# Four interleaved attention layers on one core: the keys of the first full layer made inside the layer, block by block

## The chip, the cores and the metric

The kernel runs on one core of one Trainium2 chip. The metric is the device time of one execution in microseconds (us); the time before is the median of three runs, 2756.83 us (2756.65 to 2759.04).

The engines are named by what they do: TensorE (PE in the profile) multiplies matrices into PSUM, ScalarE (ACT) takes the exps, VectorE (DVE) moves results out of PSUM and does small arithmetic, GpSimd (POOL) masks and squares, SyncE (SP) issues every transfer between memory and the core's own SBUF.

## What is computed

Four layers in turn, each a layer norm, an attention and a residual sum on x of 2048 rows by 512. Layers 0 and 2 (weights A) attend to a window of 256 keys, layers 1 and 3 (weights B) to all 2048. There are 32 heads of 16 columns.

```python
def layer(x, wqkv, wo, window):          # the reference, cut
    h = layernorm(x)
    q, k, v = heads(h @ wqkv)            # 32 heads x 2048 x 16
    scores = einsum("hqd,hkd->hqk", q, k) * 16 ** -0.5
    if window:
        scores = where(0 <= i - j < 256, scores, -1e9)
    return x + merge(softmax(scores) @ v) @ wo
x = layer(x, A_wqkv, A_wo, True)         # layer 0
x = layer(x, B_wqkv, B_wo, False)        # layer 1
x = layer(x, A_wqkv, A_wo, True)         # layer 2
x = layer(x, B_wqkv, B_wo, False)        # layer 3
```

## The kernel before

**Tiles.** The 2048 rows are four chunks of 512 (`NQ`, index c). The 32 heads are eight quads of four (`NQD`, index qd); two quads are one head tile of 128 columns (`NHT` = 4, index t or ht). Attention takes one quad and one chunk of queries at a time. In a full layer that is 16 key steps of two exps each (`attn_full`); a step's scores go to PSUM (line 727), ScalarE takes the exp (L735), and the value products follow a step or two later (L779). In a windowed layer it is three steps of two exps (`attn_win`, L731 and L812).

**Where operands lie.** Projected keys and queries go to scratch in memory (kf for full layers, kw for windowed ones, qs for queries), and attention loads them from there: qt, the queries of a quad, at L748, and kt, its keys in two halves, at L752. One row of each is a shift that keeps the exp in range. It comes from sums of squares: a projected tile is squared on GpSimd (sq, L521), a small matmul adds the squares by head (`squares`), and from that come, for keys, a maximum per chunk (km, L562) and then one shift row per head over all four chunks (mk in `key_shift`, L602), for queries the rows m (L575, L576). So a quad's attention needs its keys of all four chunks with their shift, and its queries with theirs.

**Side work.** All projections of later chunks and layers run as side work between attention steps. A `Work` is a generator with a cost and what it depends on; a `Side` holds the list for a stretch, paces it against the number of steps, and `finish()` runs whatever is left. A whole projection of keys, queries, values or outputs of a chunk is 48 matmuls of 128x512, four tiles of twelve; one head tile's keys or queries ("a quarter") are twelve; values of half the heads are 24 of 128x512 in work. In a full layer the pools leave one PSUM tile, b, for all side work, each matmul is split into eight small ones of 64x32, and VectorE evicts it in two passes (`join`). `share` doles out side work there: a budget per step, and a lag that falls by 0.42 us a step, with at most two matmuls at a time. `soon`, `drain` and `pend` order what VectorE does after a tile.

**The order of the work.** TensorE's order is the order of the code; in full layers VectorE's too. SyncE issues its transfers in the order in which the scheduler put them, each once what it reads is there and its buffer is free. Qt has two buffers, kt three halves.

**Layer 0 to 1, before.** Side work in layer 0 makes all keys of layer 1 for chunks 0 to 2 and the queries of chunk 0 (`side0`). The tail after layer 0's last attention (`tails`, `lasts`) makes the queries of chunk 1, the keys of chunk 3 and what is left of the values. Then `key_shift` writes the shift of all heads, and layer 1 runs its 32 quads (chunk by chunk, eight quads each) without a block in which anything of layer 1 has to be waited for, but for the upper half of the values, due before quad 4 of chunk 0. Layer 3 already does otherwise: it goes by head tiles, and in each block of two quads makes the next head tile's keys and queries (K3, Q3, shift3).

Of the kernel before, what the change touches and what calls it, by code (L numbers as in the profile page):

```python
# [19 lines left out]
P = 128  # L20
# [169 lines left out]
def fast_path(ctx, tc, flag, a_x, a_wqkv, a_wo, b_wqkv, b_wo, out):  # L190
# [21 lines left out]
    WT, ST, pend = {}, {}, []  # L212
    VQ, vt_ = [deque() for _ in range(4)], [0.0]
# [15 lines left out]
    def soon(chain, us, f):  # L229

        if PH["full"]:
            VQ[chain].append((clock[0], us, f))
        else:
            f()

    def drain(upto=None):

        if upto is not None:
            for q in VQ[:upto]:
                while q:  # L240
                    vec(q[0][1])
                    q.popleft()[2]()
            return
        while vt_[0] <= clock[0] + 0.2:
            q = next((q for q in VQ if q), None)
            if q is None:
                return
            vec(q[0][1])
            q.popleft()[2]()
# [179 lines left out]
    def norm(l, c, xs, tail=False):  # L429

        mv, y, nb, out = ST[l, c][1], [], [], []

        def scales():
            y.append(rsqrt(nc, vp, f"{l}_{c}", mv[:, :, 1]))
# [4 lines left out]
        def parts(i):  # L439
            xn = vp.tile([P, D], F32, name=f"xn{l}_{c}_{i}", tag="xn", bufs=1)  # L440
# [201 lines left out]
    def wo(l, c, tail):  # L642
# [4 lines left out]
        for i in range(4):  # L647
# [11 lines left out]
            yield -MM if PH["full"] else -12 * MM  # L659
        if PH["full"]:  # L660
            yield from norm(l + 1, c, xs, tail)

    def wo_part(c, t):
# [6 lines left out]
        for i in range(4):  # L670
# [7 lines left out]
            nc.sync.dma_start(out[0, k * P:(k + 1) * P, :] if t == NHT - 1 else xd[k], xs[i])  # L678
            yield -MM

    def epilogue(l, c, qd, a):
# [25 lines left out]
        def parts():  # L707
            o = vp.tile([P, QC], F32, name=f"o{n}", tag="o", bufs=1)
            nc.vector.transpose(o, OT.pop(t).rearrange("p b u d -> p (b u d)"))
            hl = O[l, c, t] = wp.tile([P, 2, QC], F16, name=f"oh{n}", tag="ohl", bufs=OB)  # L710
# [4 lines left out]
        if u:  # L715
            soon(1, 1.2, parts)
# [103 lines left out]
    class Work:  # L820
# [34 lines left out]
        proj = property(lambda self: self.name is not None and self.name[0] in ("K", "Q", "K3", "Q3"))  # L855
# [27 lines left out]
    class Side:  # L883
# [65 lines left out]
        def share(self):  # L949

            self.budget = min(self.budget + max((self.cost - self.spent) / max(self.steps - 3 - self.k, 1), self.least), 0.75)
            self.lag = max(self.lag - 0.42, -0.3)
# [5 lines left out]
            while (self.q and clock[0] >= PH["free"] and self.budget >= MM / 2 and (self.lag < 0.25 or self.budget > 0.45)  # L958
                   and self.spent - s0 < 1.5 * MM):
# [26 lines left out]
    def attention(l, works):  # L986
# [5 lines left out]
        for t in range(NHT if l == 3 else 1):  # L992
            for c in range(NQ):
                qds = range(2 * t, 2 * t + 2) if l == 3 else range(NQD)
                if l == 1:

                    sd = sd or Side(NT * NQD // 2, works[0], works[1], 0.33)
                    while ("Q", 1, c) not in DONE:
                        sd.one(True)
                    settle()  # L1000
                else:
                    sd = Side((3 if win else NT) * len(qds), works[t * NQ + c], works[t * NQ + c + 1], 0.34 if l == 3 and t < 2 else 0.0)
                ops = load(l, c, qds[0])
                for qd in qds:
                    if (l, c, qd) == (1, 0, NQD // 2):
                        sd.finish()
                        sd = Side(NT * NQD * NQ - NT * NQD // 2, works[1], works[2], 0.33)
                    nxt = load(l, c, qd + 1) if qd + 1 in qds else None
                    a = acc[qd % 2 if win else 0]
                    began, u = clock[0], 0  # L1010
# [22 lines left out]
                if l != 1 or c == NQ - 1:  # L1033
                    sd.finish(l == 3 and (t, c) != (NHT - 1, NQ - 1))
                if not win:
                    settle()
# [14 lines left out]
    def K3(c, ht, act=False):  # L1051
        return Work(later(keys, 3, c, act, ht), PK / 4, ("K3", c, ht), [("T", 3, c)], True, ring=not act)

    def Q3(c, ht, act=False, after=()):
        return Work(later(queries, 3, c, act, ht), PK / 4, ("Q3", c, ht), [("T", 3, c), *after], True, ring=not act)

    def shift3(ht):
        def gen():
            key_shift(3, ht)
            yield -1e-6  # L1060
        return Work(gen(), 0.0, ("S3", ht), [("K3", c, ht) for c in range(NQ)])
# [81 lines left out]
    def side0(c):  # L1143
# [4 lines left out]
        if c == 2:  # L1148
            return [F(*[(kf, True, k, k + 1) for k in range(NQ)]), K(0, 3), OO(0, 1), Q(0, 3), VV(0, 3), K(1, 0), T(1, 1)]
        return [F(*[(qs[1, k], False) for k in range(NQ)]), K(1, 1), OO(0, 2), VV(1, 0, True, (0,)), T(1, 2), K(1, 2), Q(1, 0)]  # L1150

    def side2(c):
        if c == 0:
            return [OO(1, 3), Q(2, 2), T(2, 3), K(2, 3)]
        if c == 1:
            return [OO(2, 0), Q(2, 3), T(3, 0), K3(0, 0, True)]
        if c == 2:
            return [OO(2, 1), VV(2, 3), T(3, 1), K3(1, 0, True)]
        return [OO(2, 2), T(3, 2), K3(2, 0, True)]
# [5 lines left out]
    def side1():  # L1165
        m = [(ty, s) for ty in range(2) for s in range(4)]
        a = [CW(*x, [("C", *y)] if y else [("Q", 1, 2)]) for y, x in zip([None] + m, m)]
        a += [Q(1, c, False) for c in (2, 3)]
        for c in range(3):
            a += [OO(1, c), T(2, c)] + ([Q(2, c - 1, False)] if c else []) + [K(2, c, False), VV(2, c, False)]  # L1170
        return a

    def side3(t, c):
        a = [Q3(c + 1, t)] if c < 3 else []
        if t < 3:
            a.append(K3(c, t + 1))
            if c == 3:
                a += [shift3(t + 1), Q3(0, t + 1)]
# [6 lines left out]
    works = [[side0(c) for c in range(NQ)], [[upper(1, c) for c in range(3)], side1()], [side2(c) for c in range(NQ)],  # L1185
             [side3(t, c) for t in range(NHT) for c in range(NQ)]]
    late = lambda l: [("N", l, 3)]
    tails = {0: [VV(1, 2, True, (0,)), OO(0, 3, True), VV(1, 1, True, (0,), late(1)), Q(1, 1, True, late(1)), T(1, 3), K(1, 3)],
             2: [VV(3, 0, True, (0,)), OO(2, 3, True), VV(3, 1, True, (0,), late(3)), VV(3, 2, True, (0,), late(3)), Q3(0, 0, True, late(3)), T(3, 3), K3(3, 0, True)]}
    lasts = {0: [VV(1, 3)], 2: [VV(3, 3, True, (0,)), VV(3, 0, True, (1,))]}  # L1190
    for l in range(4):
        if l % 2 == 0:
            attention(l, works[l] + [tails[l]])
            all_of(tails[l], lasts[l])
            key_shift(l + 1, 0 if l else None)
# [45 lines left out]
```

## Time and profile before

| | us |
|---|---|
| median of three runs | 2756.83 |
| the profiled execution, own time | 2759.5 |
| its span | 2757.7 |
| TensorE busy (91%) | 2496.1 |
| ScalarE busy (86%) | 2362.9 |
| VectorE busy (40%) | 1094.9 |
| GpSimd busy (19%) | 515.8 |

The profile is one execution; its own time lies 1.8 us above its span, and 2.7 us above the median. Layer 0's attention runs from 54 to 437 us of the span, its tail to 495.5; layer 1 to 1447; layer 2 to 1727 and its tail to 1783.6; layer 3 to 2738. Rows of the timeline give start, length, engine, line, operation, tiles and in brackets the idle time before it and what ended it; "x12" are twelve instructions merged. A busy TensorE is not at its peak, since matmuls overlap; what one costs is read from start to start.

### The profile page before, as it was taken

What the parts mean: (1) busy time and instruction counts of PE and PEld (TensorE: products, weight loads), DVE (VectorE), ACT (ScalarE), POOL (GpSimd) and SP (SyncE); (2) the same over time, 40 slices, a digit from 0 to 9 for tenths busy, and PEclk for the clock granted to TensorE, in tenths of its full rate; (3) what the DMA queues carried; (4) which work ended last, traced back from release to release, by engine and by line L of the source; (5) the groups of instructions that cost most, each with busy time, mean ns of one, the idle gap of its engine ahead of it and who ended that gap; (6) DMA issues with size and microseconds to landing.
All of it is one profiled execution on the core that took longest, in us unless ns stands there. A gap on an engine that the chain in (4) does not pass through costs nothing.

```text
span 2757.7 us, 112292 instructions
## 1 busy us (share of the span) xinstructions
PE 2496.1 (91%) x50513; PEld 1100.3 (40%) x50513; DVE 1094.9 (40%) x2314; ACT 2362.9 (86%) x2683; POOL 515.8 (19%) x1074
## 2 busy tenths in 40 slices
PE   7888989999989999999998898899899999998987
PEld 3233334444433344444443333534444444433332
DVE  5564554122343335325326566323333333333333
ACT  4556654899999999999995667399999999999997
POOL 1445552001000000100105678100000000000000
PEclk9999999999999999999999999999999999999999
DMA  8888856322342224324225565623232333333332
GB/s 286 226 241 240 244 178 191 96 83 82 100 120 79 86 93 137 102 78 126 93 73 169 157 181 143 175 72 109 84 107 90 98 97 104 112 104 123 114 120 103
DMA packets 335035, 359.67 MB, mean 130 GB/s; under 512 B 113616, under 2 KB 250320, under 8 KB 328144
## 3 DMA queue, kind: packets, MB, share of 16 engines
q1 hardware_dynamic: 334544, 352.40, 42.3%
q8 instruction: 397, 6.50, 1.0%
q14 instruction: 94, 0.77, 0.1%
HBM read 239.60 MB, written 96.99 MB: 122 GB/s over the span
## 4 chain that ended last, share of the span: by engine, by line
ACT 56%; PE 23%; issue 11%; DVE 5%; DMA 3%; POOL 2%; SPq 0%; ACTq 0%; DVEq 0%; POOLq 0%
ACT e L735 55%; PE b L402 10%; PE acc L812 3%; PE acc L779 3%; PE bs L402 2%; PE s L731 2%; PE s L727 2%; PE b L399 1%; POOL e L802 1%; POOL e L805 1%; DMA qt<-qs 1%; DMA kt<-kw 0%; DMA wr<-in_A_wo_dram 0%; DVE ot L694 0%; DMA w<-wd 0%
## 5 line engine op out<-in xcount | busy, mean ns | idle before, releaser
L735 ACT ACTIVATE e<-s 128x1024 f32<-128x1024 f32 (+2 forms) x2432 | 2238.8, 1058 | 121.0 <-PE s L731 95.3
L779 PE MATMUL acc<-e,vt 64*17 64x512 f32 x16384 | 1085.0, 590 | 1.3 <-issue 1.3
L727 PE MATMUL s<-qt,kt 64*32 64x512 f16 x16384 | 849.0, 380 | 130.4 <-ACT e L735 106.6
L727 PEld LDWEIGHTS <-kt 64*32 64x32 f16 x16384 | 406.7, 89 | 944.2 <-issue 868.8
L779 PEld LDWEIGHTS acc<-e,vt 64*17 64x17 f32 x16384 | 280.5, 92 | 61.1 <-issue 1.5
L805 POOL TENSOR_SCALAR_AFFINE_SELECT e<-e 128x256 f32<-128x256 f32 x512 | 224.9, 446 | 196.5 <-ACT e L735 195.4
L802 POOL TENSOR_SCALAR_AFFINE_SELECT e<-e 128x256 f32<-128x256 f32 x448 | 198.1, 449 | 114.1 <-ACT e L735 112.3
L712 POOL TENSOR_TENSOR oh<-o,oh 128x512 f16<-128x512 f32 x31 | 36.1, 1165 | 938.1 <-DVE oh L711 884.8
L812 PE MATMUL acc<-e,vt 128*17 128x384 f32 (+2 forms) x2816 | 204.7, 396 | 5.3 <-POOL e L802 4.0
L731 PE MATMUL s<-qt,kt 64*128 64x384 f16 (+2 forms) x1408 | 129.0, 280 | 64.0 <-ACT e L735 38.2
L415 DVE TENSOR_SCALAR sa<-acc 128x512 f32<-128x512 f32 x64 | 44.3, 692 | 335.4 <-PE acc L779 335.4
L402 PE MATMUL b<-xc,w 128*128 128x512 f16 x696 | 166.1, 390 | 7.0 <-DMA w<-wd 5.8
L677 DVE SCALAR_TENSOR_TENSOR x<-b,x 128x512 f32<-128x512 f32 x122 | 83.9, 688 | 193.0 <-PE b L399 189.8
L402 PEld LDWEIGHTS <-w 128*128 128x128 f16 x816 | 77.4, 100 | 122.8 <-issue 35.8
L521 POOL TENSOR_TENSOR sq<-sp 128x512 bf16<-128x512 f16 x28 | 41.0, 1463 | 442.2 <-DVE sp L515 427.6
L506 ACT ACTIVATE sp<-b 128x512 f16<-128x512 f32 x58 | 34.7, 598 | 103.3 <-PE b L402 91.2
L731 PEld LDWEIGHTS <-kt 64*128 64x128 f16 x1408 | 54.4, 94 | 167.6 <-issue 137.0
L521 POOL TENSOR_TENSOR sq_h<-sp_h 128x512 bf16<-128x512 f16 x27 | 40.1, 1484 | 409.8 <-DVE sp_h L515 409.8
L399 PE MATMUL b<-wo,oh 64*32 64x512 f16 x2592 | 109.9, 376 | 6.2 <-DVE x L677 3.1
L399 PE MATMUL b<-xc,w 64*32 64x512 f16 x2688 | 110.9, 376 | 3.0 <-DVE j L416 2.3
L399 PE MATMUL b<-xc,w_h 64*32 64x512 f16 x2592 | 104.4, 376 | 4.1 <-DVE km L562 3.9
L415 DVE TENSOR_SCALAR j_h<-b 128x512 f32<-128x512 f32 x27 | 18.7, 691 | 218.7 <-PE b L399 187.6
(136 smaller groups left out, 1874.8 us busy)
## 6 DMA issues: line engine op xcount, KB each, us to landing
kt<-kf SPq DMA_DIRECT2D x128, 512.0 KB
qt<-qs SPq DMA_DIRECT2D x128, 256.0 KB
xd<-x SPq DMA_DIRECT2D x96, 256.0 KB
x<-xd SPq DMA_DIRECT2D x96, 256.0 KB
w<-wd SPq DMA_DIRECT2D x22, 1024.0 KB
kt<-kw SPq DMA_DIRECT2D x64, 256.0 KB
qs<-sp SPq DMA_DIRECT2D x48, 256.0 KB
wo<-wd SPq DMA_DIRECT2D x12, 1024.0 KB
```

The costliest lines, as they stand in the source:

```text
L399: nc.tensor.matmul(ps[g:g + 32, r], a[k, g:g + 32], b[k], start=(i == 0), stop=(i == len(pairs) - 1), skip_group_check=True)
L402: nc.tensor.matmul(ps, a, b, start=(i == 0), stop=(i == len(pairs) - 1))
L415: nc.vector.tensor_scalar(dst, ps[0], scale, None, op0=ALU.mult)
L521: nc.gpsimd.tensor_tensor(sq, sp[:, 0], sp[:, 0], ALU.mult)
L677: nc.vector.scalar_tensor_tensor(xs[i], p, 1 / WS, xs[i], op0=ALU.mult, op1=ALU.add)
L727: nc.tensor.matmul(ps[g:g + 32, h], kt[R * h:R * h + R, pr, kc + g:kc + g + 32], qt[R * h:R * h + R, pr], start=True, stop=True, skip_grou ...
L731: nc.tensor.matmul(ps[:, h, s0:s0 + wd_], kt[R * h:R * h + R, pr, kc:kc + P], qt[R * h:R * h + R, pr, qc:qc + wd_], start=True, stop=True)
L735: nc.scalar.activation(e[:, :, w0:w1], ps[:, :, w0:w1], AF.Exp, scale=SCALE)
L779: nc.tensor.matmul(acc[r][32 * h:32 * h + DH + 1, :], V[l, qd // 4, j // 8][k, j % 8, 4 * (qd % 4) + h, :], es_[h // 2][k, h % 2, :], star ...
L802: nc.gpsimd.affine_select(v, v, pattern=[[0, 2], [-1, P]], compare_op=ALU.is_gt, fill=0.0, base=0, channel_multiplier=1)
L805: nc.gpsimd.affine_select(v, v, pattern=[[0, 2], [1, P]], compare_op=ALU.is_ge, fill=0.0, base=0, channel_multiplier=-1)
L812: nc.tensor.matmul(a[32 * h:32 * h + DH + 1, q * P:(q + nb) * P], V[l, (4 * c + j) // 4][:, j % 4, 4 * qd + h, :], es_[h // 2][:, h % 2, s ...
```

## The change

- Layer 0's side work makes only head tile 0 of layer 1's keys (KH), and only head tile 0 of the queries of chunk 0 (QH). The tail makes head tile 0 of chunk 3's keys, no queries of chunk 1, and in their place the upper value halves of chunks 0 to 2 and the lower of chunk 3.
- Layer 1's chunk 0 becomes four blocks of two quads. In blocks 0 to 2 the side work is `first1`: the next head tile's keys of all four chunks, their shift, and its queries of chunk 0; in block 1 the upper value half of chunk 3 too. Each of these blocks ends with `finish()`, and the next block's loads are placed after it.
- The queries of chunk 1 are made from block 3 of chunk 0 on, the first of the list `side1`, and waited for before chunk 1.
- Value chunk 2 of layer 2 is made in layer 2's chunk 0 instead of layer 1.
- In `share` the lag falls by 0.48 us a step instead of 0.42, down to -0.4 instead of -0.3, and up to three matmuls may go at a time; this holds for layer 3 as well.
- `soon` may hold back the output rows (oh) until one of their five buffers is free (`OL`, `OFREE`).

```diff
-            self.lag = max(self.lag - 0.42, -0.3)
+            self.lag = max(self.lag - 0.48, -0.4)
...
-                   and self.spent - s0 < 1.5 * MM):
+                   and self.spent - s0 < (1.5 if self.lag > 0.1 else 2.5) * MM):
...
+        elif l == 1:
+            blocks = [(t, 0, range(2 * t, 2 * t + 2)) for t in range(NHT)] + [(NHT - 1, c, range(NQD)) for c in range(1, NQ)]
...
-                    sd = sd or Side(NT * NQD // 2, works[0], works[1], 0.33)
-                    while ("Q", 1, c) not in DONE:
-                        sd.one(True)
-                    settle()
+                    if n < NHT - 1 or c == 0:
+                        sd = Side(NT * 2 if n < NHT - 1 else NT * (2 + 3 * NQD), works[n], works[n + 1], 0.33)
+                    if c:
+                        while ("Q", 1, c) not in DONE or pend and PH["busy"]:
+                            sd.one(True)
+                        settle()
...
-                if l != 1 or c == NQ - 1:
-                    sd.finish(l == 3 and (t, c) != (NHT - 1, NQ - 1))
+                if l != 1 or n < NHT - 1 or c == NQ - 1:
+                    sd.finish(l == 3 and n < NHT * NQ - 1)
...
-            return [F(*[(kf, True, k, k + 1) for k in range(NQ)]), K(0, 3), OO(0, 1), Q(0, 3), VV(0, 3), K(1, 0), T(1, 1)]
-        return [F(*[(qs[1, k], False) for k in range(NQ)]), K(1, 1), OO(0, 2), VV(1, 0, True, (0,)), T(1, 2), K(1, 2), Q(1, 0)]
+            return [F(*[(kf, True, k, k + 1) for k in range(NQ)]), K(0, 3), OO(0, 1), Q(0, 3), VV(0, 3), KH(1, 0, 0, True), T(1, 1)]
+        return [F(*[(qs[1, k], False) for k in range(NQ)]), KH(1, 1, 0, True), OO(0, 2), VV(1, 0, True, (0,)), T(1, 2), KH(1, 2, 0, True), QH(1, 0, 0, True)]
...
-            return [OO(1, 3), Q(2, 2), T(2, 3), K(2, 3)]
+            return [OO(1, 3), Q(2, 2), VV(2, 2), T(2, 3), K(2, 3)]
...
+    def KH(l, c, ht, act=False):
+        return Work(later(keys, l, c, act, ht), PK / 4, (f"K{l}", c, ht), [("T", l, c), ("P", 1, 1)], True, ring=not act)
+
+    def QH(l, c, ht, act=False, after=()):
+        return Work(later(queries, l, c, act, ht), PK / 4, (f"Q{l}", c, ht), [("T", l, c), ("P", 1, 0), *after], True, ring=not act)
...
+    def first1(t):
+        return [KH(1, c, t) for c in range(NQ)] + [SH(1, t), QH(1, 0, t)] + ([upper(1, 3)] if t == 2 else [])
...
-    tails = {0: [VV(1, 2, True, (0,)), OO(0, 3, True), VV(1, 1, True, (0,), late(1)), Q(1, 1, True, late(1)), T(1, 3), K(1, 3)],
+    tails = {0: [VV(1, 2, True, (0,)), OO(0, 3, True), VV(1, 1, True, (0,), late(1)), VV(1, 0, True, (1,), late(1)), VV(1, 1, True, (1,), late(1)), T(1, 3), KH(1, 3, 0, True)],
...
-    lasts = {0: [VV(1, 3)], 2: [VV(3, 3, True, (0,)), VV(3, 0, True, (1,))]}
+    lasts = {0: [VV(1, 3, True, (0,)), VV(1, 2, True, (1,))], 2: [VV(3, 3, True, (0,)), VV(3, 0, True, (1,))]}
```

What this does to the engines' orders, at three places. The first is TensorE at the end of block 0, between quad 1 and quad 2 of chunk 0. In a name such as s1_0_1_15_1 the digits are layer, chunk, quad, key step and half; w1_1_3_h1 are key weights of layer 1 for chunk 3 and head tile 1, w1_0_0_h1 query weights for chunk 0, sq1_1_3_h1 the squares of that key tile. Each row stands for the run of equal rows that it begins. Before:

```order
L727 MATMUL s1_0_1_15_1_7351<-qt1_0_1_5728,kt1_0_1_1_5732 32x512
L399 LDWEIGHTS xc1_1_3334
L399 MATMUL b1_5721<-wv1_1_1_0_5767,xc1_1_3334 32x256
...
L727 LDWEIGHTS kt1_0_2_0_6498
L727 MATMUL s1_0_2_0_0_7394<-qt1_0_2_6496,kt1_0_2_0_6498 32x512
```

After:

```order
L740 MATMUL s1_0_1_15_1_6793<-qt1_0_1_5484,kt1_0_1_1_5488 32x512
...
L406 MATMUL b1_5477<-xc1_3_5129,w1_1_3_h1_6030 32x512
...
L552 MATMUL b1_5477<-sq1_1_2_h1_1_6653,hsum_86 32x512
...
L552 MATMUL b1_5477<-sq1_1_3_h1_1_6886,hsum_86 32x512
...
L406 MATMUL b1_5477<-xc1_0_2371,w1_0_0_h1_6423 32x512
...
L552 MATMUL b1_5477<-sq1_0_0_h1_1_7003,hsum_86 32x512
...
L740 MATMUL s1_0_2_0_0_7025<-qt1_0_2_7013,kt1_0_2_0_7015 32x512
```

Between the two quads' scores there now stand 72 small matmuls of the last key tile, the squares of two key tiles, all 96 of the query tile, and its squares; before, there were 24 small matmuls of a value tile. At the end of quad 5 it is the same without the 72. At the end of quad 3 it is so too, with 384 value matmuls (four half-width tiles) between the query tile and its squares; and between chunks 0 and 1 there are eight matmuls of the last query tile of chunk 1 and four squares.

The second place is SyncE's queue at the loads of quad 2. Before (kt and qt are the loads, wv value weights):

```order
L752 DMA kt1_0_1_1_5732<-kf_96 128x2x1024
L748 DMA qt1_0_2_6496<-qs1_0_101 128x2x512
L752 DMA kt1_0_2_0_6498<-kf_96 128x2x1024
L370 DMA wv1_2_1_0_6824<-wd1_2_111 128x8x256
L752 DMA kt1_0_2_1_6500<-kf_96 128x2x1024
```

After (mk is the key shift, m the query shift, sp the projected rows):

```order
L613 DMA kf_96<-mk1_1_6898 8x4x512
L765 DMA kt1_0_2_0_7015<-kf_96 128x2x1024
L765 DMA kt1_0_2_1_7017<-kf_96 128x2x1024
L765 DMA kt1_0_3_0_7021<-kf_96 128x2x1024
L377 DMA w1_1_2_h2_7079<-wd1_1_110 128x8x128
L538 DMA qs1_0_101<-sp1_0_0_h1_1_7000 128x1024
L539 DMA qs1_0_101<-sp1_0_0_h1_1_7000 128x512
L597 DMA qs1_0_101<-m1_0_1_7009 8x512
L761 DMA qt1_0_2_7013<-qs1_0_101 128x2x512
L761 DMA qt1_0_3_7019<-qs1_0_101 128x2x512
```

Quad 2's queries now stand right behind the stores of what they load, and its keys right behind the store of their shift, where before nothing near them wrote what they read.

The third place is VectorE at the end of quad 3 after the change (j is the evicted query tile, vt the values, m the shift rows, sa the quad's sum of outputs):

```order
L423 SCALAR_TENSOR_TENSOR j1_0_0_h2_2_8562<-b1_5477,j1_0_0_h2_2_8562 128x512
L422 TENSOR_SCALAR vt1_1_1_5413<-b1_5477 128x16x16
L423 SCALAR_TENSOR_TENSOR vt1_1_1_5413<-b1_5477,vt1_1_1_5413 128x16x16
...
L524 CAST sp1_0_0_h2_2_8957<-j1_0_0_h2_2_8562 128x512
L525 TENSOR_TENSOR sp1_0_0_h2_2_8957<-j1_0_0_h2_2_8562,sp1_0_0_h2_2_8957 128x512
L584 TENSOR_SCALAR m1_0_2_8966<-b1_5477 32x512
L585 SCALAR_TENSOR_TENSOR m1_0_2_8966<-b1_5477,m1_0_2_8966 32x512
L422 TENSOR_SCALAR sa1_0_3_9021<-acc0_81 128x512
```

Here the pair of vt rows comes four times in a row, between the query tile's eviction and its cast to two halves; before, two such pairs stood ahead of the same quad's sa, and no query tile.

More of the change, by code (lines that the diff above doesn't have):

```diff
@@ L240, in drain @@
                 while q:
-                    vec(q[0][1])
-                    q.popleft()[2]()
+                    while q[0][2] and not q[0][2]():
+                        PH["side"].one(True)
+                    give(q)
             return
         while vt_[0] <= clock[0] + 0.2:
-            q = next((q for q in VQ if q), None)
+            q = next((q for q in VQ if q and (q[0][2] is None or q[0][2]())), None)
             if q is None:
                 return
-            vec(q[0][1])
-            q.popleft()[2]()
+            give(q)
     def turns(chain, *ops):
@@ L659, in wo @@
             yield -MM if PH["full"] else -12 * MM
+        OFREE.update((l, c, t) for t in range(NHT))
         if PH["full"]:
```

72 lines of the change are left out of this document (40 added, 32 removed).

## The prediction

> **What bounds the kernel now.** I read the busy time of each stretch first, with stretches cut where the exps of a chunk begin and end. Columns: length, ScalarE's exp busy time with its count, granted TensorE clock, DMA share, GB/s.
>
> ```profile
> 244.80:338.90 94.10, 47.60 (x49) 1.00 0.81 237
> 338.90:436.90 98.00, 47.24 (x48) 0.97 0.61 185
> 436.90:495.50 58.60, 0.00 (x0) 1.00 0.70 208
> 495.50:732.40 236.90, 235.54 (x256) 1.00 0.23 76
> ...
> 1448.40:1524.10 75.70, 36.17 (x48) 0.95 0.58 176
> 1524.10:1597.00 72.90, 45.99 (x49) 1.00 0.58 170
> 1597.00:1668.00 71.00, 45.69 (x48) 1.00 0.55 159
> ...
> 1727.10:1783.60 56.50, 0.00 (x0) 0.97 0.67 190
> 1783.60:2737.90 954.30, 943.97 (x1024) 1.00 0.33 102
> ```
>
> The first three rows are query chunks 2 and 3 of layer 0 and its tail, in which no exp runs; then chunk 0 of layer 1; then chunks 0, 1, 2 and the tail of layer 2; last, all of layer 3. In windowed layers ScalarE's exps fill half the time; in full layers they fill all of it. The groups and waits of layer 1 (495 to 1447 us) say the same:
>
> ```profile
> L735 ACT ACTIVATE e<-s 128x1024 f32<-128x1024 f32 x1024 | 943.8, 1074 | 7.7 <-PE s L727 7.1
> ```
>
> 1024 exps in 943.8 us, 0.92 us each, idle 7.7 us in the whole layer. So a full layer is bound by exps, and the one thing that lengthens it is a stretch without one. What bounds chunk 3 of layer 0 is TensorE; what it waited for there, for how long in all, how often, and the longest, is
>
> ```profile
> PE b L402 <- DMA w<-wd: 5.8, 1, 5.8
> PE s L731 <- ACT e L735: 2.1, 3, 1.0
> ```
>
> 7.9 us of 98. What work costs on TensorE shows in the tail of layer 0 (two value tiles of twelve matmuls each) and in a stretch of layer 3:
>
> ```profile
> 489.59 2.75 PE L402 MATMUL bs<-wv,xc 128*128 128x512 f16 x12
> 492.18 2.75 PE L402 MATMUL b<-wv,xc 128*128 128x512 f16 x12
> ```
> ```profile
> 2163.08 0.53 PE L727 MATMUL s<-qt,kt 64*32 64x512 f16 x8
> 2163.29 1.17 PE L779 MATMUL acc<-e,vt 64*17 64x512 f32 x16
> 2164.15 0.53 PE L727 MATMUL s<-qt,kt 64*32 64x512 f16 x8
> ```
>
> From start to start, twelve full matmuls take 2.59 us (0.216 each). In a full layer eight small ones, which do one full one's work, take 0.21, and the sixteen value passes of a key step 0.86. A key step (two exps, 1.84 us) so needs 2 x 0.21 + 0.86 = 1.29 us of TensorE and leaves 0.55 for side work.
>
> **The change: what it takes off layer 0.** Chunk 2 loses three quarters of a key chunk, 36 of 240 full matmuls: 36 x 0.216 = 7.8 us (0 if another engine then binds). Chunk 3 loses 108 of 216, 23.3 us, and may lose the 5.8 us wait for weights. It is then left with 108, as chunks 1 and 2 of layer 2 have, and these took 72.9 and 71.0: 98.0 - 72 = 26. I take 25 (15 to 28). The tail:
>
> ```profile
> 454.65 1.47 PE L402 MATMUL bs<-wv,xc 128*128 128x256 f16 x12
> ...
> 471.79 2.75 PE L402 MATMUL bs<-xc,w 128*128 128x512 f16 x12 [1.14 <-DMA xc<-xh]
> ...
> 494.86 0.62 PE L727 MATMUL s<-qt,kt 64*32 64x512 f16 x16
> ```
> ```profile
> 1765.56 4.45 PE L402 MATMUL bs<-xc,w_h 128*128 128x512 f16 x12 [3.79 <-DMA x<-xd]
> 1769.94 0.39 PE L546 MATMUL b<-sq_h,hsum 128*32 128x512 bf16 x1
> ...
> 1783.07 0.63 PE L727 MATMUL s<-qt,kt 64*32 64x512 f16 x16 [0.75 <-DMA kt<-kf]
> ```
>
> After the last output tile (454.65) come three value halves, 72 x 0.216 = 15.6 us, to 470.2; the transposed activations arrive at 471.8 as before; the key quarter ends at 474.4. In layer 2's tail the first scores came 13.1 us after the key tile's end (1769.94 to 1783.07), so here at 487.5 instead of 494.9: 7.4 us won (2.1, if it only gets as short as layer 2's tail of 56.5, to 10). Layer 2's chunk 0 gets the moved value chunk: 48 x 0.216 = 10.3 us lost (5 to 12, as some of it may fall into waits). Sum of the windowed layers: 7.8 + 25 + 7.4 - 10.3 = **30 us won** (5 to 43).
>
> **What it puts on layer 1.** The moved projections are 48 x 4.75 matmuls, less 48 for value chunk 2 and 48 for the upper value halves that go to the tail: 132 more, 28 us of TensorE, against 512 x 0.55 = 280 us of slack. As work they are hidden. What isn't is the end of a block. The order of TensorE (shown above) has the query quarter of the next head tile wholly behind the last scores of quads 1, 3 and 5: its 96 small matmuls, the squares and then at once the next quad's scores. ScalarE has two exps left, 1.8 us, and then nothing until query rows have gone to memory and come back. This chain is in the trace, though hidden: the same query quarter in layer 3 (VectorE, GpSimd, SyncE), the one in layer 2's tail (SyncE), and the kernel's first query load (SyncE, TensorE).
>
> ```profile
> 1988.08 0.69 DVE L415 TENSOR_SCALAR j_h<-b 128x512 f32<-128x512 f32 x1 [9.18 <-PE b L399]
> ...
> 1999.36 0.68 DVE L575 TENSOR_SCALAR m<-b 32x512 f16<-32x512 f32 x1 [0.49 <-PE b L543]
> 2000.08 0.68 DVE L576 SCALAR_TENSOR_TENSOR m<-b,m 32x512 f16<-32x512 f32 x1
> ```
> ```profile
> 1990.16 1.48 POOL L521 TENSOR_TENSOR sq_h<-sp_h 128x512 bf16<-128x512 f16 x1 [13.51 <-DVE sp_h L515]
> ```
> ```profile
> 2000.79 0.28 SPq L588 DMA_DIRECT2D qs<-m  x1
> 2002.53 0.37 SPq L748 DMA_DIRECT2D qt<-qs  x1
> ```
> ```profile
> 1771.07 0.31 SPq L588 DMA_DIRECT2D qs<-m  x1
> ...
> 1774.47 0.37 SPq L748 DMA_DIRECT2D qt<-qs  x1
> 1774.93 0.32 SPq L604 DMA_DIRECT2D kf<-mk  x1
> ...
> 1777.53 1.41 SPq L752 DMA_DIRECT2D kt<-kf  x3
> ```
> ```profile
> 50.31 0.52 SPq L761 DMA_DIRECT2D qt<-qs  x1
> ```
> ```profile
> 53.49 0.82 PE L731 MATMUL s<-qt,kt 64*128 64x384 f16 x4 [4.27 <-DMA qt<-qs]
> ```
> ```profile
> 1783.61 4.69 ACT L735 ACTIVATE e<-s 128x1024 f32<-128x1024 f32 x5 [0.87 <-PE s L727]
> 1789.31 1.02 ACT L735 ACTIVATE e<-s 128x1024 f32<-128x1024 f32 x1 [1.01 <-PE s L727]
> ```
>
> From the tile's last matmul: 3.6 us until GpSimd has its square (1988.08 to 1991.64), 0.4 for the squares' matmul, 1.4 for the two shift rows m (1999.36 to 2000.76), 1.7 to 3.4 until m is in memory and the load goes out, 3.2 to the first scores, 0.5 to the exp (1783.07 to 1783.61): 10.9 to 12.6, I take 11.8. Ahead of the query tile stands the last key tile's maximum:
>
> ```profile
> L562 DVE TENSOR_REDUCE km<-b 32x1 f32<-32x1024 f32 x12 | 14.7, 1223 | 30.5 <-PE b L543 30.5
> ...
> L415 DVE TENSOR_SCALAR vt<-b 128x256 f32<-128x256 f32 x12 | 5.1, 422 | 67.1 <-PE b L399 67.1
> ```
>
> It holds the one PSUM tile that the query matmuls need: 3.6 + 0.4 + 1.2 and 0.2 of handing over, 5.4 us from the key tile's end. Counted from the block's last scores:
> - after quad 5 the key tile ended 1.3 us earlier, in step 14. -1.3 + 5.4 + 2.6 (query tile) + 11.8 - 1.8 = **16.7 us** without an exp;
> - after quad 1, 72 key matmuls are left, so it ends at +2.2: **20.2 us**;
> - after quad 3, as after quad 5, but four half-width value tiles, each 1.3 us of matmuls, 0.85 of eviction (two passes of 0.42) and some 0.2 of handing over, stand on VectorE ahead of the query's cast: + 4 x 2.35 = **26.1 us**;
> - at chunk 1 only eight matmuls are left, but four m stores instead of one go out ahead of the load: 0.4 + 11.8 + 1.3 - 1.8 = **11.7 us**.
>
> Together 74.7. The key rows come back sooner: 4.1 + 0.5 + 2.6 (1774.93 to 1777.53) + 5.5 (1777.53 to 1783.07) = 12.7 us after the last scores of quad 5, against 18.5 for the query. The floor, with nothing ahead of the query tile: 3 x (2.6 + 10.9 - 1.8) + 11 = 46. The ceiling, with C at 12.6 and m waiting behind a key load for another 5.5 us at three ends: 94. A restart costs about the 1.0 us that stood after layer 2's tail (1789.31), so 4 in all (0 to 8). Inside the blocks 58 steps hold 24 side matmuls, 0.64 + 1.29 = 1.93 against 1.84 us; the next step is lighter and takes most of it back: 2.5 us (0 to 6). Layer 1 so loses **81 us** (46 to 108). Layer 3's new pace puts no work at a block end: 0, within 3 either way.
>
> On the restart, the row at 1765.56 shows twelve matmuls in 4.45 us behind an idle 3.79, against 2.75 elsewhere. [...]
>
> [...]
>
> **Sum:** 2757.7 - 30 + 81 = 2809 us of span. The profiled execution took 2759.5, 1.8 outside its span, and lies 2.7 above the median of 2756.8, so by the median 2756.8 + 51 = **2808**.
>
> **Rivals.**
> *Block ends are hidden (faster).* Layer 3 already has such blocks, and across its second head tile's start, near 2023 us, exps run on unbroken:
>
> ```profile
> 1995.04 50.82 ACT L735 ACTIVATE e<-s 128x1024 f32<-128x1024 f32 x55
> ```
>
> If SyncE's early loads hid layer 1's ends as well, only 2.5 us would stand against 30: 2729. It decides at 30 us of waits in all. Against it: in layer 3 that query tile was evicted at 1988, 35 us ahead of its use, here it isn't even begun. 4%.
> *Short waits, full gain.* Waits near the floor (50 to 60 with restarts) and 40 us won: 2767 to 2780. It needs reductions and squares to run beside the query tile, though they share one PSUM tile. 9%.
> *Layer 0 doesn't shorten.* DMA share there is 0.61 to 0.81 against 0.55 to 0.58 in layer 2; if fills and stores bind, half the gain goes and m's stores wait too: 2757 - 12 + 95 = 2840. 9%.
> *My forecast*, waits 60 to 90 and gains 22 to 36: 78%, 2780 to 2825.
>
> The range takes in the forecast and most of the slower rival: 2780 to 2838. What a measurement can tell from no change is about 0.2%, 5.5 us. Faster 4%, within 2%, slower 94%.
>
> **What would show it.** In the changed profile: chunk 3 of layer 0 near 73 us and its tail near 51; layer 2's chunk 0 near 86; in layer 1 exactly four long idle times of ScalarE, each ended by scores that waited for the load of qt, in the order 20, 26, 17, 12 us; chunks 1 to 3 and layer 3 as now. I am wrong if these idle times come to under 45 us, if scores wait for kt instead of qt, or if layer 0's chunk 3 stays over 85.

## The result, and the profile after

The changed kernel takes 2818.65 us, the median of four runs (2817.12 to 2825.53); the kernel before, run beside it, 2757.93. The ratio is 1.0222 (95% interval 1.0202 to 1.0243): slower by 61 us. The profiled execution has a span of 2817.3 us, 59.6 more than before.

The stretches are cut where the exps of a chunk begin and end (length, ScalarE's exp time and count, granted TensorE clock, DMA share, GB/s): chunks 2 and 3 and the tail of layer 0, chunk 0 and chunks 1 to 3 of layer 1, the way from layer 1's last exp through layer 2's chunk 0, and layer 3. First the kernel before (its chunk 0 of layer 1, 236.9 us, stands in the prediction), then the changed one.

```profile
244.80:339.00 94.20, 47.62 (x50) 1.00 0.82 237
339.00:436.80 97.80, 47.20 (x48) 0.97 0.61 185
436.80:495.50 58.70, 0.02 (x1) 1.00 0.70 208
...
732.40:1447.00 714.60, 708.26 (x769) 1.00 0.33 100
1447.00:1524.20 77.20, 36.29 (x50) 0.96 0.59 178
1783.60:2737.80 954.20, 943.94 (x1024) 1.00 0.33 102
```
```profile
245.20:335.00 89.80, 46.88 (x50) 1.00 0.72 215
335.00:405.80 70.80, 45.94 (x48) 1.00 0.66 182
405.80:458.00 52.20, 0.03 (x1) 1.00 0.65 185
458.00:783.90 325.90, 236.81 (x257) 0.91 0.25 78
783.90:1500.90 717.00, 709.50 (x768) 1.00 0.34 103
1500.90:1578.80 77.90, 36.70 (x49) 1.00 0.66 193
1839.80:2799.50 959.70, 946.52 (x1024) 1.00 0.34 103
```

The windowed side won nearly what it should: 94.2 to 89.8, 97.8 to 70.8 and 58.7 to 52.2, together 37.9 us of the 40.2 expected. Chunk 0 of layer 1 went from 236.9 to 325.9 us with the same 256 exps. Where these 89 us lie, ScalarE's timeline shows: four exps that came after a long idle time, at the ends of quads 1, 3, 5 and of the chunk.

```profile
539.45 1.02 ACT L748 ACTIVATE e<-s 128x1024 f32<-128x1024 f32 x1 [22.39 <-PE s L740]
...
632.58 1.02 ACT L748 ACTIVATE e<-s 128x1024 f32<-128x1024 f32 x1 [32.53 <-PE s L740]
...
713.29 1.02 ACT L748 ACTIVATE e<-s 128x1024 f32<-128x1024 f32 x1 [19.18 <-PE s L740]
...
783.86 1.02 ACT L748 ACTIVATE e<-s 128x1024 f32<-128x1024 f32 x1 [9.85 <-PE s L740]
```

Together 84.0 us. What the scores before these exps waited for is in TensorE's waits in layer 1 (who waited for whom, us in all, times, longest):

```profile
...
PE s L740 <- DMA qt<-qs: 23.3, 4, 6.0
PE b L552 <- POOL sq_h L530: 10.3, 3, 3.7
PE b L552 <- DVE km L571: 6.3, 3, 2.1
PE b L406 <- DVE km L571: 4.5, 4, 1.3
PE b L406 <- DVE vt L423: 3.8, 4, 1.0
PE b L406 <- issue: 2.7, 1, 2.7
...
```

Left out are the short waits for ScalarE's exps (34.9 us in 104 waits, the longest 1.0; before the change 43.7 in 119 over the layer, the longest 1.1), the usual pace of a full layer here, and smaller rows. The scores waited four times for the load of the queries; and ahead of it, in the order of the chain, TensorE waited for the key maximum and for GpSimd's square. The chain itself at the end of quad 1, on TensorE and SyncE:

```profile
515.50 0.41 PE L740 MATMUL s<-qt,kt 64*32 64x512 f16 x8
515.71 2.14 PE L406 MATMUL b<-xc,w_h 64*32 64x512 f16 x72
519.39 0.39 PE L552 MATMUL b<-sq_h,hsum 64*32 64x512 bf16 x2 [1.54 <-DVE j_h L423]
521.88 0.61 PE L552 MATMUL b<-sq_h,hsum 64*32 64x512 bf16 x2 [2.10 <-DVE km L571]
523.80 4.88 PE L406 MATMUL b<-xc,w_h 64*32 64x512 f16 x96 [1.31 <-DVE km L571]
532.37 0.61 PE L552 MATMUL b<-sq_h,hsum 64*32 64x512 bf16 x2 [3.69 <-POOL sq_h L530]
538.69 0.63 PE L740 MATMUL s<-qt,kt 64*32 64x512 f16 x8 [5.71 <-DMA qt<-qs]
539.07 1.95 PE L792 MATMUL acc<-e,vt 64*17 64x512 f32 x16
```
```profile
524.33 0.29 SPq L613 DMA_DIRECT2D kf<-mk  x1
526.16 1.42 SPq L765 DMA_DIRECT2D kt<-kf  x3
...
534.45 0.29 SPq L597 DMA_DIRECT2D qs<-m  x1
535.81 0.88 SPq L761 DMA_DIRECT2D qt<-qs  x2
```

From the last scores of one block (515.50) to the first of the next (538.69), 23.2 us in which one step waits for the one before. In 14.4 of them TensorE stood still: the five waits in brackets behind the key tile's row. Two rows matter for what follows. The query tile's 96 matmuls took 4.88 us, where twelve times the prediction's 0.216 us comes to 2.6; the granted clock was 0.56 in that time. The first value products after the wait took 1.95 us, where they take 1.05 elsewhere.

### The profile page after: what moved, and what is told of

It reads as the page before. It is cut to its first block, busy times and chain, and to the rows that moved or that the text cites. A ratio compares the mean times of both kernels' runs of the same rounds, so it can differ in the third digit from the quotient of the medians.

```text
span 2817.3 us, 113675 instructions
## 1 busy us (share of the span) xinstructions
PE 2503.4 (89%) x51168; PEld 1117.7 (40%) x51168; DVE 1143.4 (41%) x2372; ACT 2352.0 (83%) x2657; POOL 543.2 (19%) x1093
## 4 chain that ended last, share of the span: by engine, by line
ACT 54%; PE 23%; issue 12%; DVE 5%; DMA 3%; POOL 2%; SPq 0%; ACTq 0%; DVEq 0%; POOLq 0%
ACT e L748 53%; PE b L409 9%; PE acc L792 3%; PE acc L825 3%; PE b L406 2%; PE s L740 2%; PE bs L409 2%; PE s L744 2%; POOL e L815 1%; DMA qt<-qs 1%; POOL e L818 1%; DVE km L571 0%; DMA kt<-kw 0%; DMA wr<-in_A_wo_dram 0%; DVE xh L457 0%
## 5 line engine op out<-in xcount | busy, mean ns | idle before, releaser
L530 POOL TENSOR_TENSOR sq_h<-sp_h 128x512 bf16<-128x512 f16 x42 | 62.2, 1482 | 601.1 <-DVE sp_h L524 601.1
L406 PE MATMUL b<-xc,w_h 64*32 64x512 f16 x4032 | 165.9, 392 | 7.9 <-DVE km L571 7.9
L422 DVE TENSOR_SCALAR j_h<-b 128x512 f32<-128x512 f32 x42 | 28.8, 686 | 343.8 <-PE b L406 283.6
L406 PE MATMUL b<-xc,w 64*32 64x512 f16 x3072 | 127.1, 376 | 0.8 <-DVE j L423 0.8
L409 PE MATMUL b<-xc,w 128*128 128x512 f16 x468 | 109.3, 384 | 1.5 <-DVE km L571 1.5
L406 PE MATMUL b<-wo,oh 64*32 64x512 f16 x2592 | 100.8, 376 | 2.2 <-DVE x L687 0.8
L409 PEld LDWEIGHTS <-xc 128*128 128x128 f16 x864 | 82.2, 98 | 51.3 <-issue 13.2
L825 PEld LDWEIGHTS acc<-e,vt 128*17 128x17 f32 x2816 | 64.2, 97 | 91.1 <-issue 53.4
```

Of the source, the lines that this page charges most:

```text
L406: nc.tensor.matmul(ps[g:g + 32, r], a[k, g:g + 32], b[k], start=(i == 0), stop=(i == len(pairs) - 1), skip_group_check=True)
L409: nc.tensor.matmul(ps, a, b, start=(i == 0), stop=(i == len(pairs) - 1))
L422: nc.vector.tensor_scalar(dst, ps[0], scale, None, op0=ALU.mult)
L530: nc.gpsimd.tensor_tensor(sq, sp[:, 0], sp[:, 0], ALU.mult)
L825: nc.tensor.matmul(a[32 * h:32 * h + DH + 1, q * P:(q + nb) * P], V[l, (4 * c + j) // 4][:, j % 4, 4 * qd + h, :], es_[h // 2][:, h % 2, s ...
```

## Experiments

My theory: what costs is the way of a block's last tile to memory and back, whichever tile it is. The main rival: the blocks hold too much work for TensorE. "Idle times" below are the four of ScalarE in chunk 0 of layer 1, in order; the changed kernel's are 22.4, 32.5, 19.2, 9.9.

**Queries early.** The queries of chunk 0 made whole in layer 0, the keys left in the blocks.

```diff
-        return [F(*[(qs[1, k], False) for k in range(NQ)]), KH(1, 1, 0, True), OO(0, 2), VV(1, 0, True, (0,)), T(1, 2), KH(1, 2, 0, True), QH(1, 0, 0, True)]
+        return [F(*[(qs[1, k], False) for k in range(NQ)]), KH(1, 1, 0, True), OO(0, 2), VV(1, 0, True, (0,)), T(1, 2), KH(1, 2, 0, True), Q(1, 0)]
...
-        return [KH(1, c, t) for c in range(NQ)] + [SH(1, t), QH(1, 0, t)] + ([upper(1, 3)] if t == 2 else [])
+        return [KH(1, c, t) for c in range(NQ)] + [SH(1, t)] + ([upper(1, 3)] if t == 2 else [])
```

> Queries of chunk 0 of layer 1 are made whole in layer 0, as before; keys stay in the blocks. Theory (what costs is the last tile's way to memory and back at a block's end): the query tile and its chain go, the last key tile's chain stays, and it is shorter. From the changed kernel's trace the key shift store goes out 8.8 us after the last scores of quad 1 and the key load 1.8 us after it; with 4 to 5.5 us for the load the idle times at the ends of quads 1, 3, 5 and chunk 0 become about 15, 15 (value tiles), 10.5 and 10 us, 50 instead of 84. Layer 0 gives back 36 matmuls, 7.8 us. Total 2788 to 2796. Rival (the blocks are too full for TensorE): 36 matmuls of some 200 in the blocks are gone, the idle times fall by a fifth: 2805 to 2815.

2785.75 us, ratio 1.0102 (1.0085 to 1.0118). ScalarE:

```profile
536.80 1.02 ACT L748 ACTIVATE e<-s 128x1024 f32<-128x1024 f32 x1 [14.29 <-PE s L740]
...
614.14 1.02 ACT L748 ACTIVATE e<-s 128x1024 f32<-128x1024 f32 x1 [15.92 <-PE s L740]
...
684.62 1.02 ACT L748 ACTIVATE e<-s 128x1024 f32<-128x1024 f32 x1 [10.14 <-PE s L740]
...
755.37 1.02 ACT L748 ACTIVATE e<-s 128x1024 f32<-128x1024 f32 x1 [9.80 <-PE s L740]
```

50.2 us instead of 84.0, as the theory had it, each within a microsecond. The fall is twice the fifth that the rival gives. Chunk 3 of layer 0 got 6.6 us longer (77.4). The total is 2 us under what I expected; 4.6 us of the gain lie in layer 3 (955.1 instead of 959.7), which the edit doesn't reach (see "Value chunk back").

**Query ahead of the last key.** The same work in another order.

```diff
-        return [KH(1, c, t) for c in range(NQ)] + [SH(1, t), QH(1, 0, t)] + ([upper(1, 3)] if t == 2 else [])
+        return [KH(1, c, t) for c in range(NQ - 1)] + [QH(1, 0, t), KH(1, 3, t), SH(1, t)] + ([upper(1, 3)] if t == 2 else [])
```

> Same work, but the query tile is made ahead of the last key tile of each block. Theory (whichever tile is last costs its chain): the idle times stay, a little shorter, about 19, 22, 17 and 10 us, now ended by the load of keys (kt) at the three block ends; total 2800 to 2808. Rival (it is the query's load alone): the three block ends lose their idle times, total 2750 to 2760.

2808.97 us, ratio 1.0183 (1.0166 to 1.02). Idle times 20.4, 24.9, 17.0, 10.1: the second is 2.9 us longer and the total 1 us more than the theory gave. On TensorE, at the end of quad 1:

```profile
520.86 2.78 PE L406 MATMUL b<-xc,w_h 64*32 64x512 f16 x96 [1.54 <-DVE j_h L423]
...
538.12 0.63 PE L740 MATMUL s<-qt,kt 64*32 64x512 f16 x8 [7.73 <-DMA kt<-kf]
```

The idle times stay and are now ended by the keys' load. It is not the query as such; the last tile costs its chain. (Here its 96 matmuls, 1.5 us behind other work, took 2.78, at a granted clock of 1.00.)

**Values in the tail.** The upper value half of chunk 3 made in layer 0's tail.

```diff
-        return [KH(1, c, t) for c in range(NQ)] + [SH(1, t), QH(1, 0, t)] + ([upper(1, 3)] if t == 2 else [])
+        return [KH(1, c, t) for c in range(NQ)] + [SH(1, t), QH(1, 0, t)]
...
-    lasts = {0: [VV(1, 3, True, (0,)), VV(1, 2, True, (1,))], 2: [VV(3, 3, True, (0,)), VV(3, 0, True, (1,))]}
+    lasts = {0: [VV(1, 3), VV(1, 2, True, (1,))], 2: [VV(3, 3, True, (0,)), VV(3, 0, True, (1,))]}
```

> The upper value half of chunk 3 is made in layer 0's tail instead of block 1. Theory (the value tiles stand on VectorE between the query tile's eviction and its cast): the idle time after quad 3 falls from 32.5 to about 19.5 us, that after quad 5's length; the tail grows by 0 to 5 us; total 2806 to 2811. Rival (quad 3's end is long for another reason, such as the transfers): idle time stays over 28, total 2817 to 2824.

2808.8 us, ratio 1.0177 (1.016 to 1.0194). After quad 3:

```profile
624.94 1.02 ACT L748 ACTIVATE e<-s 128x1024 f32<-128x1024 f32 x1 [18.19 <-PE s L740]
```

18.2 instead of 32.5: four value tiles between the query's eviction and its cast cost 14.3 us. The tail grew from 52.2 to 58.9, more than I had allowed, so of the 14.3 us some 8 came through by the spans (2817.3 to 2809.0) and 9.9 by the medians.

**Value chunk back.** Value chunk 2 of layer 2 in layer 1, as before the change.

```diff
-            return [OO(1, 3), Q(2, 2), VV(2, 2), T(2, 3), K(2, 3)]
+            return [OO(1, 3), Q(2, 2), T(2, 3), K(2, 3)]
...
-            a += [K(2, c, False)] + ([VV(2, c, False)] if c < 2 else [])
+            a += [K(2, c, False), VV(2, c, False)]
```

> Value chunk 2 of layer 2 is made in layer 1 again. Theory (in layer 2's chunk 0 it filled idle time of TensorE and so cost about 1 us, and in layer 1 it is hidden): layer 2's chunk 0 at 75.7 us again, total within 2 us of the changed kernel, 2816 to 2821. Rival (the 10.3 us of my forecast): total 2808.

2809.86 us, ratio 1.0191 (1.0171 to 1.0211), outside what I expected, on the side of the rival; but not where the rival has it. From layer 1's last exp to layer 2's chunk 1, and layer 3:

```profile
1497.90:1574.80 76.90, 36.25 (x49) 0.98 0.64 193
1836.60:2790.20 953.60, 944.97 (x1024) 1.00 0.34 104
```

76.9 instead of 77.9: the moved chunk costs 1.0 us in layer 2, not 10.3. Its idle times are the changed kernel's within 0.7 us. Most of the rest is layer 3, 953.6 instead of 959.7, and there nothing was changed: this kernel and the changed one have in layer 3 the same instructions on TensorE, ScalarE, VectorE and SyncE, in the same order. So have five other experiments, the first but for its last output tiles; in the order in which they stand here (queries early, query ahead of the last key, values in the tail, pace alone, clock kept up) layer 3 took 955.1, 960.6, 959.2, 955.8 and 959.2 us. One layer thus differs by up to 7 us from profile to profile with nothing changed in it; from what, no run shows. So this run's 8.8 us under the changed kernel are for the most part no price of the moved chunk, and a difference of some 5 us between two totals proves little here.

**Pace alone.** The kernel before, with the new pace.

```diff
-            self.lag = max(self.lag - 0.42, -0.3)
+            self.lag = max(self.lag - 0.48, -0.4)
...
-                   and self.spent - s0 < 1.5 * MM):
+                   and self.spent - s0 < (1.5 if self.lag > 0.1 else 2.5) * MM):
```

> The kernel before with only the new pace (lag 0.48 down to -0.4, up to three matmuls at a time) in both full layers. Theory A (layer 3's 5.5 us more in the profile of the changed kernel are the pace): layers 1 and 3 each 3 to 6 us longer, total 2763 to 2769. Theory B (they differ from one execution to the next, since two experiments with the same pace had 955.0 and 953.5 us there): within 3 us of before, 2755 to 2761.

2764.46 us, ratio 1.0015 (1.0005 to 1.0026), some 4 us more. Neither theory fits whole: the total is A's, but in the profile layer 3 took 955.8 (954.2 before) and layer 1 955.0 (951.5), from the first exp to the end of the last. In layer 3, whose instructions here are the changed kernel's, 955.8 against its 959.7 speaks for B. The pace costs little; in which layer, one profile each doesn't show.

**Clock kept up.** Sixteen full matmuls of zeros ahead of the first scores after each wait; what they write is overwritten.

```diff
+        if PH.pop("fresh", False):
+            for _ in range(16):
+                nc.tensor.matmul(ps[:, 0], ones[:, :P], zeros, start=True, stop=True)
...
+                PH["fresh"] = l == 1 and n > 0 and c < 2
                 ops = load(l, c, qds[0])
```

> The changed kernel with 16 extra full matmuls of zeros ahead of the first scores after each of the four idle times, in the time in which TensorE waits for the load; they write the scores' own PSUM tile, which is then overwritten. Theory (TensorE restarts with a slow clock after the wait, which costs 1.4 to 2.2 us in each first quad, 7.2 in all): idle time inside these quads falls to under 0.7 us each, granted clock of chunk 0 rises, total 4 to 6 us less than the changed kernel, if the extra matmuls (8 slow and 8 fast ones, 5.1 us) fit in the wait of 5.7 to 6.0. Rival (the restart costs because values and scores are queued, whatever the clock): idle inside stays at 1.4 to 2.2 each.

2809.78 us, ratio 1.0181 (1.0161 to 1.0202). After quad 1, and chunk 0 as a whole:

```profile
533.83 6.19 PE L736 MATMUL s<-zeros,ones 128*128 128x512 f16 x16
540.11 0.41 PE L743 MATMUL s<-qt,kt 64*32 64x512 f16 x8
540.33 1.05 PE L795 MATMUL acc<-e,vt 64*17 64x512 f32 x16
```
```profile
459.20:776.40 317.20, 236.67 (x256) 0.96 0.26 82
```

The value products behind the wait take 1.05 us again instead of 1.95, the idle time inside the next quad falls from 1.4 to 0.1, and from 2.2 and 2.1 to 0.1 after quad 3 and the chunk; after quad 5 it stays (1.6). The granted clock of the chunk rises from 0.91 to 0.96. So TensorE does restart slowly behind a wait of 5.7 us. The 5.1 us expected for the zeros were the author's estimate; after quad 1 they took 6.19, and of the prediction's twelve matmuls in 4.45 us nine ran at a granted clock of 0.50 (1766.17 to 1769.58 in the profile before). After quad 5 the zeros took only 3.63 us, and TensorE then waited again:

```profile
705.40 0.41 PE L743 MATMUL s<-qt,kt 64*32 64x512 f16 x8 [3.67 <-DMA qt<-qs]
```

Behind these 3.67 us the value products were slow once more (1.28 and 1.99); the waits left after quad 3 and the chunk, 2.04 and 2.54, did no harm. The total fell by 8.9 us, more than the 4 to 6 expected, as the idle times themselves also fell (22.5, 29.1, 17.5, 9.7). After quad 3 the 2.7 us that TensorE's waits gave to "issue" and the slow value tiles behind them are missing; after quad 5 the query tile took 2.78 us instead of 5.20. Both lie ahead of the zeros of their own block end, and why they went isn't shown.

**Combined.** Each chain gets six steps or more before it is needed, but for the one at quad 1: queries of chunk 0 and keys of chunk 0 whole in layer 0, the blocks of key work shorter and the last one begun early, half of the four value tiles in the tail, and the new pace in layer 1 alone.

```diff
-            self.lag = max(self.lag - 0.48, -0.4)
+            self.lag = max(self.lag - (0.48 if PH["l"] == 1 else 0.42), -0.4 if PH["l"] == 1 else -0.3)
...
-                   and self.spent - s0 < (1.5 if self.lag > 0.1 else 2.5) * MM):
+                   and self.spent - s0 < (1.5 if self.lag > 0.1 or PH["l"] != 1 else 2.5) * MM):
...
-                    if n < NHT - 1 or c == 0:
-                        sd = Side(NT * 2 if n < NHT - 1 else NT * (2 + 3 * NQD), works[n], works[n + 1], 0.33)
+                    if n < NHT - 2:
+                        sd = Side(26, works[n], works[n + 1], 0.33)
+                    elif n < NHT - 1:
+                        sd = Side(NT * (4 + 3 * NQD), works[n] + works[n + 1], works[n + 2], 0.45)
+                    elif c == 0:
+                        while ("S1", 3) not in DONE:
+                            sd.one(True)
...
-                if l != 1 or n < NHT - 1 or c == NQ - 1:
+                if l != 1 or n < NHT - 2 or c == NQ - 1:
...
-        return Work(gen(), 0.0, (f"S{l}", ht), [(f"K{l}", c, ht) for c in range(NQ)])
+        return Work(gen(), 0.0, (f"S{l}", ht), [(f"K{l}", c, ht) for c in range(1 if l == 1 else 0, NQ)])
...
-            return [F(*[(kf, True, k, k + 1) for k in range(NQ)]), K(0, 3), OO(0, 1), Q(0, 3), VV(0, 3), KH(1, 0, 0, True), T(1, 1)]
-        return [F(*[(qs[1, k], False) for k in range(NQ)]), KH(1, 1, 0, True), OO(0, 2), VV(1, 0, True, (0,)), T(1, 2), KH(1, 2, 0, True), QH(1, 0, 0, True)]
+            return [F(*[(kf, True, k, k + 1) for k in range(NQ)]), K(0, 3), OO(0, 1), Q(0, 3), VV(0, 3), K(1, 0), T(1, 1)]
+        return [F(*[(qs[1, k], False) for k in range(NQ)]), KH(1, 1, 0, True), OO(0, 2), VV(1, 0, True, (0,)), T(1, 2), KH(1, 2, 0, True), Q(1, 0)]
...
-            a += [OO(1, c), T(2, c)] + ([Q(1, c + 2, False)] if c < 2 else []) + ([Q(2, c - 1, False)] if c else [])
+            a += [OO(1, c), T(2, c)] + ([Q(1, c + 2, False, [("O", 1, c, NHT - 1)])] if c < 2 else []) + ([Q(2, c - 1, False)] if c else [])
...
-        return [KH(1, c, t) for c in range(NQ)] + [SH(1, t), QH(1, 0, t)] + ([upper(1, 3)] if t == 2 else [])
+        return [KH(1, c, t) for c in range(1, NQ)] + [SH(1, t)] + ([upper(1, 3, range(2, 4))] if t == 2 else [])
...
-    lasts = {0: [VV(1, 3, True, (0,)), VV(1, 2, True, (1,))], 2: [VV(3, 3, True, (0,)), VV(3, 0, True, (1,))]}
+    lasts = {0: [VV(1, 3, True, (0,)), VV(1, 2, True, (1,)), VV(1, 3, True, (1,), (), range(2))], 2: [VV(3, 3, True, (0,)), VV(3, 0, True, (1,))]}
```

> What the runs so far point to: every chain to memory and back gets seven or more steps before it is needed. Queries of chunk 0 and keys of chunk 0 of layer 1 whole in layer 0, so that three key tiles a block are left; half of the upper values of chunk 3 in the tail, half behind block 1's keys; queries of chunk 1 begin in block 2 and no block end stands between; the query projections of chunks 2 and 3 wait for chunk 0's outputs; old pace outside layer 1. Theory (it was the place of the last tiles, not the amount of work): chunk 3 of layer 0 at 77.4 as in the run with early queries, the tail 53 to 57, in chunk 0 of layer 1 one idle time of about 6 us after quad 1 (its squares come at step 14) and under 2 us at the other three ends; total 2740 to 2750, faster than before. Rival (blocks with key work are slow whatever their order): idle times of 8 us or more at two or more ends, total over 2760.

2749.59 us, ratio 0.9963 (0.9949 to 0.9976): faster than before by 0.4%. Chunk 3 of layer 0, the tail and chunk 0 of layer 1; then the one long idle time left, on ScalarE and on TensorE:

```profile
338.90:415.90 77.00, 46.38 (x48) 1.00 0.64 190
415.90:471.80 55.90, 0.00 (x0) 1.00 0.68 181
471.80:719.30 247.50, 236.40 (x257) 0.99 0.27 84
```
```profile
536.37 1.02 ACT L748 ACTIVATE e<-s 128x1024 f32<-128x1024 f32 x1 [5.56 <-PE s L740]
```
```profile
535.61 0.63 PE L740 MATMUL s<-qt,kt 64*32 64x512 f16 x8 [6.02 <-DMA kt<-kf]
```

As expected, 5.6 us after quad 1 and at most 1.5 at the other ends, with key work still in blocks 0 to 2. It is less work, though, three key tiles a block and no query tile of chunk 0, and at this pace less work also ends earlier, so the total alone doesn't tell place from amount. TensorE's waits do: at the end of quad 1 it had no work left ahead of the next scores and stood 6.0 us waiting for the keys' load, and in the changed kernel it stood still for 14.4 of 23.2 us. And the run with the query ahead of the last key had the same amount of work, and its waits went over to the tile that was then last. So what costs is the way to memory and back behind the last tile; the amount counts in that it sets when that tile comes.

**One more key.** The combined kernel with the key quarter of chunk 1, head tile 1, in layer 0 as well.

```diff
-        return [F(*[(qs[1, k], False) for k in range(NQ)]), KH(1, 1, 0, True), OO(0, 2), VV(1, 0, True, (0,)), T(1, 2), KH(1, 2, 0, True), Q(1, 0)]
+        return [F(*[(qs[1, k], False) for k in range(NQ)]), KH(1, 1, 0, True), KH(1, 1, 1, True), OO(0, 2), VV(1, 0, True, (0,)), T(1, 2), KH(1, 2, 0, True), Q(1, 0)]
...
-        return [KH(1, c, t) for c in range(1, NQ)] + [SH(1, t)] + ([upper(1, 3, range(2, 4))] if t == 2 else [])
+        return [KH(1, c, t) for c in range(2 if t == 1 else 1, NQ)] + [SH(1, t)] + ([upper(1, 3, range(2, 4))] if t == 2 else [])
```

> The combined kernel with one more key quarter (chunk 1, head tile 1) made in layer 0, so that block 0 has two key tiles and its last squares come at step 7 of quad 1 instead of 14. Theory (idle time at a block's end is what is left of the chain, which starts at those squares): the one idle time left, 5.6 us and 2.4 inside the next quad, goes to under 1 us; layer 0 pays 12 matmuls, 2.6 us; chunk 0 of layer 1 at 238 to 240 us, total 2743 to 2747. Rival (that wait is the value tiles or the transfers of block 0, not the late squares): idle time after quad 1 stays over 4 us, total 2751 to 2754.

2744.31 us, ratio 0.9949 (0.9936 to 0.9963). Chunk 0, and all that ScalarE waited for scores in layer 1:

```profile
477.10:718.60 241.50, 236.45 (x256) 0.99 0.27 83
```
```profile
ACT e L748 <- PE s L740: 8.0, 11, 1.5
```

No idle time over 1.5 us is left in layer 1: the last key squares, seven steps earlier, hide the chain. Chunk 0 is 1.5 us longer than expected, and chunk 3 of layer 0 and its tail took 80.4 and 56.9 us, 4.4 more than in the combined kernel instead of 2.6. So it is 14 us under the kernel before, but not shown to be faster than the combined one: the intervals of the two ratios overlap, and the profiled spans are 2744.7 and 2744.3 us.

## Why the prediction was right

It forecast 2808 (2780 to 2838), slower by waits at block ends; 2818.65 was measured, and the waits stand where it put them, in the order of length that it gave, each ended by the load of the queries. Term by term, from the profiles (the rows add to 59.8 of the 59.6 us):

| term | forecast | measured |
|---|---|---|
| layer 0, chunk 2 | -7.8 | -4.4 |
| layer 0, chunk 3 | -25 | -27.0 |
| tail | -7.4 | -6.5 |
| layer 2, chunk 0 | +10.3 | +0.7 |
| four idle times | +74.7 | +84.0 |
| restarts | +4 | +7.2 |
| layer 1, steps in between | +2.5 | +0.3 |
| layer 3 | 0 | +5.5 |

The restarts are the idle times inside the quads behind the four waits, 1.4, 2.2, 1.5 and 2.1 us. The last lies in chunks 1 to 3, whose 717.0 us against 714.6 are so all but explained; in chunk 0 the idle times and three restarts make up the whole 89 us.

The mechanism was right. That the total missed by only 11 us is in part luck: five terms came out dearer than forecast, by 22 us in all, while layer 2's chunk 0, where the working was wrong, came out 10 us cheaper and two others 4. Two sums in the working are slightly off and move nothing: the most that the windowed layers could win adds to 41, not 43 (7.8 + 28 + 10 - 5), and the chain's parts to 10.8 to 12.5.

- **The idle times** were expected as 20.2, 26.1, 16.7, 11.7 and measured as 22.4, 32.5, 19.2, 9.9. What was too small is the query tile's own time. I took 2.6 us for its 96 matmuls; behind the waits for the squares and the key maximum they took 4.88, 4.47 and 5.20 after quads 1, 3 and 5, in the first case at a granted clock of 0.56, and in the experiment with the query first, with no such waits ahead of it, 2.78 at 1.00. What was too large is the rest: the shift rows were in memory 1.4 us after their store was issued (534.45 to 535.81) and the scores began 2.9 after the load (535.81 to 538.69), less than the 1.7 to 3.4 and the 3.2 that I took.
- **After quad 3** the value tiles cost 14.3 us (the run with the values in the tail), not 9.4. Part of that is the same slow clock (0.50 granted from 614.9 to 620.3 us); 2.7 us of it, the wait put to "issue", no engine accounts for.
- **Layer 2's chunk 0** is the step that failed: I charged all 48 matmuls to the path and said that only some might fall into waits. TensorE's waits there, before and after:

```profile
PE s L731 <- ACT e L735: 6.7, 13, 1.1
PE s L731 <- DMA qt<-qs: 3.8, 1, 3.8
```
```profile
PE s L744 <- ACT e L748: 3.6, 6, 0.9
```

  10.5 us of waits became 3.6, so most of the work went into time in which TensorE stood still; the run with the chunk moved back confirms 1.0 us. The prediction shows the waits of layer 0's chunk 3, but not those of this stretch.
- **Layer 0's chunk 2** gave 4.4 of 7.8 us; why the rest didn't come wasn't tried.
- **Restarts** cost 7.2 us, not the 4 taken from the 1.0 us behind layer 2's tail. The granted clock was 0.50 in the first 2.3 us after quad 1's wait (538.69 to 541.00), and the run with the extra matmuls shows the clock as the cause: with it kept up (0.96 in chunk 0 instead of 0.91), three of the four are gone.
- **Layer 3** was put at 0, within 3. Its 5.5 us aren't shown to be the change's: in runs with the same instructions there it took 953.6 to 960.6 us. From what it differs stays open.
- **The rivals.** That SyncE's early loads would hide the ends is refuted: the loads stood in the queue and waited for the stores of what they load (after quad 1 the queries' load went out at 535.81, 1.4 us behind the last store). That the waits would be near their floor of 46 is refuted by 84. That layer 0 wouldn't shorten is refuted by 37.9 us.

## What to carry to other kernels

Moving work from a stretch where its engine is the bound to one where it has slack is only half of the sum: the work's last result has a latency, and where the next step reads it through memory that latency needs as many steps of cover as it is long, here 10 to 20 us or six to eleven key steps, by estimate from 1.84 us a step and the idle times of the changed kernel and the run with early queries (9.8 to 22.4 us where no value tiles stood in between). Look in the program's order for what stands between a block's last step and the next block's first; if it is a projection and a store and its load, it isn't side work any more. Before charging moved work to the path of its new place, read that place's waits: it may be free there.

## What the runs showed of the hardware

- TensorE's slow start: 96 small matmuls behind waits took 4.88 us at a granted clock of 0.56, against 2.78 at 1.00, and sixteen passes of values 1.95 against 1.05. Sixteen full matmuls issued into a wait of some 6 us took it away; where 3.67 us of waiting followed them it came back, where 2.04 or 2.54 followed it didn't.
- The slow start isn't the same each time: behind the same waits of 2.1 and 1.3 us after quad 5 the 96 matmuls took 5.20 us in the changed kernel and 2.78 in the run with the clock kept up.
- In the run with the query first, three loads of keys, 512 KB each (half of a quad's keys), were issued together, and the first scores began 4.0 us later (534.11 to 538.12), where layer 2's tail had 5.5.
- With the same instructions in the same order, an exp-bound layer took 953.6 to 960.6 us in different runs.
